# Attention and two MLPs on one core: cluster chain and normalisation one tile sooner, weight conversions in five tiles of twelve

## Chip, cores, metric

One NeuronCore of a Trainium2 chip. The metric is the device time of one execution in microseconds, the median of several runs. Engines are named as in the profile: PE (TensorE matmuls), PEld (its weight loads), DVE (VectorE), ACT (ScalarE), POOL (GpSimd), SP (SyncE, here the only queue that issues DMAs).

## What is computed

```python
# q, k, v: (2, 8, 768, 64); centroids: (8, 16, 64)
q_assign = argmax(einsum('bhsd,hcd->bhsc', q_n, c_n))      # nearest of 16 clusters
k_assign = argmax(einsum('bhsd,hcd->bhsc', k_n, c_n))
scores = where(q_assign[..., None] == k_assign[..., None, :], q @ k.T / 8, -1e9)
x = softmax(scores) @ v                                    # -> (1536, 512)
x = relu(x @ w_in) ** 2 @ w_out                            # 512 -> 2048 -> 512
p = domain_probs / domain_probs.sum(-1)
out = sum over 4 experts of p[:, e] * (relu(x @ w1[e]) @ w2[e])
```

All of it is fp32. Matmuls work on pairs of a rounded value and its remainder (names ending in h and l, or hi and lo), so most operands are made twice.

## The kernel before

The attention is one loop over 96 tiles `g`: 16 heads of 6 tiles, a tile being 128 queries of a head. Twelve tiles make a pair of heads, and a tile is named below by its number and by its place in the twelve (tile 61 is place 1 of its pair, tile 55 is place 7). In each tile PE makes the scores of the tile after next (`S`, L593), transposes the probabilities of the present one in two halves (`T0`, `T1`, L626) and multiplies earlier ones with v (L640, L642). DVE takes the row maximum of the scores (`nb`, L602) and the remainder of each transposed half (`ptl`, L632, two a tile); ACT does the exponential (L613) and the rounded copy of each half (`pth`, L631). The transposed halves go through two PSUM buffers, so T0 of a tile waits for the first `ptl` of the tile before it.

Two strings in `ORDER` (one for even tiles, one for odd) set the order in which a tile's pieces are emitted, and every engine runs its instructions in that order. Beside the base work a tile has places for other work:

- **The slots X1 and X2** take PE work of the cluster chain of the next pair of heads, at places given in `AT` (`START` for the first). Its steps: four transposes of k and q ("t": L364, evacuated by ACT to `kqf`, L371, then split by POOL into `nkh`/`nkl` and `nqh`/`nql`, L52 and L373); two cluster scores, one for each half of the 768 rows ("a", first two: four matmuls each from nkh, nkl, nqh, nql, L414, copied by ACT to `ys`, L420); two turns (transposes of ys, L430, reduced by DVE to `A`, L435); and the one-hot transposes (`pair_hot`, L481). All these use one PSUM buffer, `ps_m`, with bufs=1. `nkh` and its three fellows have one SBUF buffer each.
- **The queue `dq`**, from which C takes one entry: two maxima on DVE (L469, L470), each followed by POOL work (L459 to L467). They make the one-hot rows that the one-hot transposes read.
- **The normalisation** of the pair that has just ended (`norm_steps`, f1 to f5): sums to reciprocals on DVE (L696, L697), a transpose (L702), a store and a broadcast load through DRAM (`rd`, `rb`, L708, L714), and POOL work (f4: L723; f5, two halves: L677, L52, L686).
- **K, the weight conversion**: one entry of `cq`, from tile 8 on, if dq is empty and the tile's place is in "turns". There are 24 entries, four blocks of six: five DVE operations on the scratch tile `cva` (L167, L170, L173, L178, L183) and one copy by ACT with a subtraction by POOL (`w0h`, L189; `w0l`, L191). `cva` has one buffer, so the first operation of a block waits for the `w0l` of the block before. When cq is empty, K loads two weight pieces (`raw`, L109) in each tile whose number is 4 modulo 6.
- **R** issues the DMAs that put the heads' operands together: `k1`, `q1`, `k2`, `q2` (`stack`, L385 and L387, copies out of nkh, nkl, nqh, nql), the one-hot rows (L498), v, and the next q and k.

After the last tile come the two MLPs, dense matmuls from L783 on.

Of the kernel before, what the change touches and what calls it, by code (L numbers as in the profile page):

```python
# [13 lines left out]
AX = mybir.AxisListType  # L14
# [10 lines left out]
    "S T0 X1 M E T1 R Y1 H0 P0 X2 C H1 L0 L1 C K Y2".split(),  # L25
    "S X1 E M T0 T1 Y1 H0 C P1 X2 R L0 H1 C L1 Y2 O K C".split()]
WARM = [12, 10, 5, 11, 3, 9]
START = {'t': [0, 0, 1, 1], 'a': [3, 3, 4, 4, 7], 'stack1': 4, 'stack': 5, 'head': 2, 'gap': 3}
AT = {"gap": 4, "stack1": (-11, -10), "stack": (-9, -9), "ohd": -7, "splitv": -3, "load": -10,
      "t": [-14, -13, -12, -11], "a": [-10, -10, -9, -8, -5], "conv": 8, "turns": (2, 6, 7, 8, 9, 10)}  # L30


@with_exitstack
def moe_attention_kernel(
# [20 lines left out]
    C = centroids.shape[1]  # L55
    NT, DM = out.shape
    E = moe2_w1.shape[0]
    NTT = S // 128
# [147 lines left out]
    with tc.manual_schedule():  # L206
# [217 lines left out]
        def pair_turn(j, half):  # L424

            def f():
                m = ps_m.tile([128, QT, 128], F32, tag="m", name="m")
                for t in range(QT):
                    c0 = half * HALF + t * 128
                    nc.tensor.transpose(m[:, t], ys[j][:, c0:c0 + 128], identf)  # L430

                def evac():
                    if half == 0:
                        ya[j] = as_p.tile([128, 4 * NTT, C], F32, tag="A", name="A")
                    nc.vector.reduce_sum(  # L435
                        out=ya[j][:, half * 4 * QT:(half + 1) * 4 * QT],
                        in_=m.rearrange("p t (g s c) -> p (t g) c s", g=4, s=2), axis=AX.X)
                    if half:
                        for _ in range(len(dq)):
                            dq.pop(0)()  # L440
                        dq.extend(pair_ops(j, ya.pop(j)))
                        for _ in range(2):
                            dq.pop(0)()
                return evac
            return f

        ys, ya = {}, {}

        def pair_ops(j, A):
            mx = as_p.tile([128, 4 * NTT, 1], F32, tag="mx", name="mx")  # L450
            mx2 = as_p.tile([128, 4 * NTT, 1], F32, tag="mx2", name="mx2")
# [3 lines left out]
            V, P = nc.vector, nc.gpsimd  # L455
# [10 lines left out]
                P.tensor_scalar(off, av[:, :, 0], 0.0, -1.0, op0=ALU.min, op1=ALU.max)  # L466
                P.tensor_scalar(oh[:, :, :, 1], off, 1.0, -NEG, op0=ALU.add, op1=ALU.mult)  # L467

            m1 = lambda: V.reduce_max(out=mx, in_=A, axis=AX.X)  # L469
            m2 = lambda: V.reduce_max(out=mx2, in_=A, axis=AX.X)  # L470
            return [m1, p1] + [lambda: None] * (AT if j > 1 else START)["gap"] + [m2, p2]

        def pair_hot(j):

            def f():
                while dq:
                    dq.pop(0)()
                om = oms[j] = as_p.tile([128, HALF], F32R, tag="ohm", name="ohm")
                m = ps_m.tile([128, HALF], F32R, tag="m", name="m")
                for a in range(QT):  # L480
                    nc.tensor.transpose(  # L481
                        m[:, a * 128:(a + 1) * 128],
                        ohs["p", j][:, 2 * a:2 * a + 2].rearrange("p t e s c -> p (t e s c)"), identr)

                def evac():
                    nc.scalar.copy(om, m.bitcast(F32))
                    hot_rows(2 * j)
                return evac
            return f
# [50 lines left out]
        def onehot_slot(i):  # L540

            def f():
                while dq:
                    dq.pop(0)()
                om = as_p.tile([128, HALF], F32R, tag="ohm", name="ohm")[0:4 * C]
                m = ps_m.tile([4 * C, HALF], F32R, tag="m", name="m")
                for a in range(QT):
# [141 lines left out]
        def norm_steps(hp):  # L689
# [36 lines left out]
            def f5(half):  # L726
                norm_scaled(hp, half, st["rb"][:, half * HALF:(half + 1) * HALF], nc.gpsimd, round_pool)

            return [[f1], [], [f2], [], [f3, lambda: f4], [], [lambda: f5(0)], [lambda: f5(1)]]

        def norm_last(hp):
            st = {}
# [339 lines left out]
        split_v(0)  # L1072
        k2hi()
        while dq:
            dq.pop(0)()
        k1lo()
        nc.gpsimd.memset(cp.bitcast(F32), 0.0)
        for e in range(2):
# [11 lines left out]
        emit_max(1)  # L1090
        sums()
        for _ in range(2):
            dq.pop(0)()
        nc.sync.dma_start(out=dp, in_=domain_probs.rearrange("(b p t) e -> p b t e", b=B, t=NTT))
        load_w(*w_loads(0)[0])

# [31 lines left out]
        cq, lq = [], []  # L1128
# [10 lines left out]
        for g in range(NU):  # L1139
# [29 lines left out]
                    f()  # L1169

            def convert():
                if g >= AT["conv"] and cq:
                    if not dq and g % (2 * NTT) in AT["turns"]:
                        cq.pop(0)()
                elif not cq and g % NTT == 4:
                    for _ in range(2):
                        lq and lq.pop(0)()

            def finish(n):
                f = end.pop(n, None)  # L1180
# [8 lines left out]
            def maximum():  # L1189
# [6 lines left out]
                "M": maximum, "P0": lambda: PV(0), "P1": lambda: PV(1),  # L1196
                "O": PO, "R": other, "T0": lambda: T(0), "T1": lambda: T(1),
                "X1": lambda: slot("Y1"), "X2": lambda: slot("Y2"),
                "C": lambda: dq and dq.pop(0)(),
                "K": convert,  # L1200
            }
            for a in ORDER[par]:
# [25 lines left out]
        f1, f2, f3, f4 = norm_last(hp)  # L1228
        f1()
        while dq:  # L1230
            dq.pop(0)()
        act = early_gemm1(1)
        whole(f2)
        act()
# [146 lines left out]
```

## Time and profile before

| | |
|---|---|
| runs, median (lowest, highest) | 1029.36 us (1028.94, 1030.99) |
| the profiled execution: its time, its span | 1029.81 us, 1028.0 us |
| PE busy, PEld busy | 1015.5 us (99%), 899.3 us (87%) |
| DVE, ACT, POOL busy | 675.7 us (66%), 530.2 us (52%), 567.0 us (55%) |
| chain that ended last | PE 85%, DVE 5%, POOL 3%, DMA 2%, ACT 2% |
| granted PE clock | full speed in all 40 slices |

The profile comes from one execution, whose span is the time from its first to its last instruction; the time of the run is 1.8 us longer. PE's busy time is modelled from starts and pipelined ends, so a PE at 99% may still be delayed; whether it is shows in the distance between the starts of matmuls. Below, the one-hot transposes of PE (L481) serve as marks: stretch 1 runs from those of tile 7 to those of tile 19, stretch 6 to those of tile 79, twelve tiles each. In the views times are microseconds from the start of the span, and what stands in brackets at the end of a row is how long its engine was idle before it and what ended that.

### The profile page before, as it was taken

How to read it: one execution, taken by the hardware profiler on the slowest of the kernel's cores; microseconds unless marked ns; L12 is line 12 of the kernel's file. 1: busy time of each engine (PE TensorE's matmuls, PEld its weight loads, DVE VectorE, ACT ScalarE, POOL GpSimd, SP SyncE). 2: the span in 40 equal slices, each digit the busy share in tenths (PEclk: the TensorE clock that was granted, in tenths of full speed). 3: DMA queues.
4: the chain of work that ended last, by engine and by line, in shares of the span. 5: the costliest groups of instructions: out<-in, count | busy, mean ns of one | idle time of the engine just before them, and what ended most of it. 6: DMA issues, size and time to landing. Idle time of an engine off the chain costs nothing.

```text
span 1028.0 us, 14886 instructions
## 1 busy us (share of the span) xinstructions
PE 1015.5 (99%) x5507; PEld 899.3 (87%) x5507; DVE 675.7 (66%) x1047; ACT 530.2 (52%) x1066; POOL 567.0 (55%) x557
## 2 busy tenths in 40 slices
PE   8999999999999999999999999999999999999998
PEld 7988899899888888888889898899888898998887
DVE  8888888889776773721265555578686565555554
ACT  6888888889565533443353343333453333333331
POOL 4467787574232222235456656667678566566550
PEclk9999999999999999999999999999999999999999
DMA  6577766863123320211012212112124122122101
GB/s 151 113 178 179 162 144 156 179 164 90 32 92 98 108 82 31 93 41 41 0 42 83 73 50 82 57 67 83 44 80 143 42 82 83 41 83 69 55 1 62
DMA packets 73745, 88.86 MB, mean 86 GB/s; under 512 B 27252, under 2 KB 50184, under 8 KB 73672
## 3 DMA queue, kind: packets, MB, share of 16 engines
q1 hardware_dynamic: 73672, 87.91, 30.5%
q8 instruction: 43, 0.70, 0.3%
q14 instruction: 30, 0.25, 0.1%
HBM read 62.58 MB, written 3.19 MB: 64 GB/s over the span
## 4 chain that ended last, share of the span: by engine, by line
PE 85%; DVE 5%; POOL 3%; DMA 2%; ACT 2%; issue 1%; SPq 1%; POOLq 0%; ACTq 0%
PE bank L954 25%; PE bank L914 22%; PE bank L807 13%; PE bank L783 4%; PE bank L784 4%; PE bank L782 4%; PE s L593 3%; PE t L626 3%; PE po L640 2%; PE po L642 2%; DVE ptl L632 1%; DVE nb L602 1%; DMA rd<-rt 1%; DMA rb<-rd 1%; POOL nql L373 1%
## 5 line engine op out<-in xcount | busy, mean ns | idle before, releaser
L954 PE MATMUL bank<-w1h,ga 128*128 128x512 f32 x768 | 269.9, 393 | 0.0
L964 DVE SCALAR_TENSOR_TENSOR x<-bank,pe_p,x 128x512 f32<-128x512 f32 x180 | 135.0, 751 | 167.7 <-PE bank L954 167.6
L914 PE MATMUL bank<-xa,w0h 128*128 128x384 f32 x896 | 228.3, 335 | 0.1
L914 PEld LDWEIGHTS bank<-xa,w0h 128*128 128x128 f32 x896 | 164.5, 188 | 17.9 <-ACT fa L925 0.5
L954 PEld LDWEIGHTS bank<-w1h,ga 128*128 128x128 f32 x768 | 144.1, 188 | 24.5
L793 POOL TENSOR_TENSOR ga<-fa,ga 128x512 fp32r<-128x512 f32 x48 | 63.2, 1318 | 177.7 <-ACT ga L792 136.7
L954 PE MATMUL bank<-w1l,ga 128*128 128x512 f32 x384 | 151.6, 395 | 0.0
L914 PE MATMUL bank<-xa,w0l 128*128 128x384 f32 x448 | 149.7, 334 | 0.0
L925 ACT COPY fa<-bank 128x384 f32<-128x384 f32 x96 | 45.5, 474 | 171.7 <-PE bank L914 171.7
L807 PE MATMUL bank<-ga,w1h 128*128 128x512 f32 x384 | 126.6, 389 | 0.0
L934 ACT ACTIVATE ga<-fa 128x384 fp32r<-128x384 f32 x96 | 50.5, 527 | 135.6 <-DVE fa L928 135.6
L883 POOL TENSOR_TENSOR w0l<-raw,w0h 128x512 fp32r<-128x512 f32 x64 | 75.0, 1195 | 81.4 <-ACT w0h L882 81.4
L901 POOL TENSOR_TENSOR w1l<-raw,w1h 128x1024 fp32r<-128x1024 f32 x32 | 77.3, 2414 | 71.3 <-ACT w1h L900 71.3
L632 DVE TENSOR_TENSOR ptl<-t,pth 128x384 fp32r<-128x384 f32 x192 | 97.8, 548 | 26.7 <-ACT pth L631 26.4
L602 DVE TENSOR_REDUCE nb<-s 128x1 f32<-128x768 f32 x96 | 91.3, 951 | 7.9 <-PE s L593 6.9
L937 DVE SCALAR_TENSOR_TENSOR ga<-fa,ga 128x384 fp32r<-128x384 f32 x96 | 90.1, 938 | 0.6 <-ACT ga L934 0.6
L631 ACT CAST pth<-t 128x384 fp32r<-128x384 f32 x192 | 84.5, 486 | 8.8 <-PE t L626 8.1
L613 ACT ACTIVATE p<-s,nb 128x768 f32<-128x768 f32 x96 | 87.7, 914 | 2.0 <-DVE nb L602 1.9
L626 PE MATMUL t<-identf,p 128*128 128x128 f32 x576 | 86.7, 276 | 1.3 <-DVE ptl L632 0.8
L593 PE MATMUL s<-k,q 80*128 80x384 f32 (+1 forms) x384 | 85.7, 344 | 2.2 <-DMA k<-ohm 1.4
L790 ACT ACTIVATE fa<-bank 128x512 f32<-128x512 f32 x44 | 26.3, 598 | 116.3 <-PE bank L784 116.3
L807 PEld LDWEIGHTS bank<-ga,w1h 128*128 128x128 f32 x384 | 72.0, 188 | 14.7
(213 smaller groups left out, 2045.1 us busy)
## 6 DMA issues: line engine op xcount, KB each, us to landing
raw<-in_moe_w_dram SPq DMA_DIRECT2D x64, 512.0 KB, 4.3
raw<-in_moe_w_in_dram SPq DMA_DIRECT2D x7, 1024.0 KB, 5.2
raw<-in_moe_w_out_dram SPq DMA_DIRECT2D x6, 1024.0 KB, 4.9
k<-nkh SPq DMA_DIRECT2D x28, 192.0 KB, 3.8
q<-nqh SPq DMA_DIRECT2D x28, 192.0 KB, 3.9
nv<-in_v_dram SPq DMA_DIRECT2D x16, 192.0 KB, 3.9
out_dram<-x SPq DMA_DIRECT2D x12, 256.0 KB, 2.1
k<-nkl SPq DMA_DIRECT2D x14, 192.0 KB, 3.3
```

The costliest lines, as they stand in the source:

```text
L593: nc.tensor.matmul(s[:, j, 0:HALF], stk[i, nq][:, t * 128:(t + 1) * 128], stk[i, nk][:, j * HALF:(j + 1) * HALF], start=first, stop=not first)
L602: nc.vector.tensor_reduce(out=nb, in_=s_ps[u][:, :, 0:HALF], axis=AX.XY, op=ALU.max, negate=True)
L613: nc.scalar.activation(p, s_ps.pop(u)[:, :, 0:HALF], AF.Exp, bias=nb_t.pop(u), accum_out=sums_t[hp][:, i % 2, t:t + 1])
L626: nc.tensor.transpose(tp[:, j], p_sb[u][:, half, j * 128:(j + 1) * 128], identf)
L631: return (lambda: nc.scalar.copy(dh, tp), lambda: nc.vector.tensor_tensor(dl, tp, dh.bitcast(F32), op=ALU.subtract))
L632: lambda: nc.vector.tensor_tensor(dl, tp, dh.bitcast(F32), op=ALU.subtract))
L807: nc.tensor.matmul(o, a, b, start=(ft == 0 and z == 0), stop=(ft == NF - 1 and z == 2))
L901: nc.gpsimd.tensor_tensor(lo, w, hi.bitcast(F32), op=ALU.subtract)
L914: nc.tensor.matmul(ps, w[:, o:o + 128], r_op(r, x)[:, kt], start=(first and kt == 0 and z == 0), stop=(kt == 1 and z == 2), skip_group_che ...
L937: nc.vector.scalar_tensor_tensor(out=g_t(n, f, t, 1), in0=h_src(n, f, t), scalar=0.0, in1=g_t(n, f, t, 0).bitcast(F32), op0=ALU.max, op1=A ...
L954: nc.tensor.matmul(o, a, w[:, f], start=(f == 0 and z == 0), stop=(f == 1 and z == 2))
L964: nc.vector.scalar_tensor_tensor(out=acc, in0=o, scalar=pc, in1=acc, op0=ALU.mult, op1=ALU.add)
```

## The change

The places of the cluster chain become 1, 2, 2, 3, 7 instead of 2, 2, 3, 4, 7: the first cluster scores go to the tile that also has the fourth transpose, the first turn to the tile of the second scores. The maxima of the queue keep to places 4 and 5. `norm_steps` drops one empty step, so that the broadcast load and f5 come one tile sooner (places 5, 7 and 8 instead of 6, 8 and 9), and f4 runs in place 6, in its slot. Conversions run at places 6 to 10 and no longer at 2. Pieces of weights are loaded at place 10, two at a time, the first four as soon as half of the conversions are done.

```diff
-AT = {"gap": 4, "stack1": (-11, -10), "stack": (-9, -9), "ohd": -7, "splitv": -3, "load": -10,
-      "t": [-14, -13, -12, -11], "a": [-10, -10, -9, -8, -5], "conv": 8, "turns": (2, 6, 7, 8, 9, 10)}
+AT = {"stack1": (-11, -10), "stack": (-9, -9), "ohd": -7, "splitv": -3, "load": -10,
+      "t": [-14, -13, -12, -11], "a": [-11, -10, -10, -9, -5], "conv": 8, "turns": (6, 7, 8, 9, 10)}
...
                     if half:
-                        for _ in range(len(dq)):
-                            dq.pop(0)()
-                        dq.extend(pair_ops(j, ya.pop(j)))
-                        for _ in range(2):
-                            dq.pop(0)()
+                        first, second = pair_ops(j, ya.pop(j))
+                        if j == 1:
+                            first()
+                            dq.extend([None] * 3 + [second])
+                        else:
+                            dq.extend([None, first, None, None, None, second])
...
-            return [[f1], [], [f2], [], [f3, lambda: f4], [], [lambda: f5(0)], [lambda: f5(1)]]
+            return [[f1], [], [f2], [f3], [f4], [lambda: f5(0)], [lambda: f5(1)]]
...
             def convert():
-                if g >= AT["conv"] and cq:
-                    if not dq and g % (2 * NTT) in AT["turns"]:
-                        cq.pop(0)()
-                elif not cq and g % NTT == 4:
+                turn = g % (2 * NTT)
+                if g >= AT["conv"] and cq and not dq and turn in AT["turns"]:
+                    cq.pop(0)()
+                if lq and turn == AT["turns"][-1] and len(cq) <= (12 if len(lq) > 4 else 0):
                     for _ in range(2):
-                        lq and lq.pop(0)()
+                        lq.pop(0)()
```

`first` is the first maximum with its POOL work, `second` the second.

**PE, tiles 61 and 62 (places 1 and 2): the first cluster scores.** In these rows `m<-nkh` to `m<-nql` are the scores of one half, `t` is T0, `s` the scores of attention. Before:

```order
L640 MATMUL po<-pth,vv 128x256
L642 MATMUL po<-ptl,vv 128x256
L593 MATMUL s<-k_2502,q_2596 128x384 x2
L593 MATMUL s<-k_2599,q_2601 128x384 x2
L626 MATMUL t<-identf,p 128x128 x3
L414 MATMUL m<-nkh,cp 128x384
L414 MATMUL m<-nkl,cp 128x384
L414 MATMUL m<-nqh,cp 128x384
L414 MATMUL m<-nql,cp 128x384
```

With the change:

```order
L651 MATMUL po<-pth,vv 128x256
L653 MATMUL po<-ptl,vv 128x256
L419 MATMUL m<-nkh,cp 128x384
L419 MATMUL m<-nkl,cp 128x384
L419 MATMUL m<-nqh,cp 128x384
L419 MATMUL m<-nql,cp 128x384
L604 MATMUL s<-k_2508,q_2605 128x384 x2
L604 MATMUL s<-k_2608,q_2610 128x384 x2
L637 MATMUL t<-identf,p 128x128 x3
```

The first scores now stand at the end of tile 61, ahead of S and T0 of tile 62. The second scores take their old place behind T0, and the first turn stands at the end of tile 62.

**POOL, the second pair (tiles 18 to 22): f4, the conversion's subtraction and f5.** `xs<-xs,xm` is f4, `rb` and `xa` are f5. Before:

```order
L723 TENSOR_TENSOR xs<-xs,xm 128x384 x2
L191 TENSOR_TENSOR w0l<-cva,w0h 128x4x128
L677 TENSOR_TENSOR rb<-rb,xs 128x384
L52 TENSOR_SCALAR xa<-rb 128x384
L686 TENSOR_TENSOR xa<-rb,xa 128x384
```

With the change:

```order
L734 TENSOR_TENSOR xs<-xs,xm 128x384 x2
L688 TENSOR_TENSOR rb<-rb,xs 128x384
L52 TENSOR_SCALAR xa<-rb 128x384
L697 TENSOR_TENSOR xa<-rb,xa 128x384
L688 TENSOR_TENSOR rb<-rb,xs 128x384
L52 TENSOR_SCALAR xa<-rb 128x128
L697 TENSOR_TENSOR xa<-rb,xa 128x128
L52 TENSOR_SCALAR xa<-rb 128x256
L697 TENSOR_TENSOR xa<-rb,xa 128x256
L191 TENSOR_TENSOR w0l<-cva,w0h 128x4x128
L52 TENSOR_SCALAR vv<-nv 128x6x64
```

`w0l` has gone from ahead of f5 to behind it, and the conversion that writes `cva` anew stands one tile later on DVE (tile 21). In the third pair `w0l` stands behind `vv` (tile 33, the next block begins in tile 34), in the fourth between the first `nkl` and the second `nkh` (tile 46), the last one in tile 66.

**DVE, tiles 62 to 64 of the sixth pair: the turns.** `A<-m` ends a turn, `mx` is the first maximum. Before:

```order
L602 TENSOR_REDUCE nb<-s 128x1
L435 TENSOR_REDUCE A<-m 128x192
L696 TENSOR_SCALAR r<-sums 128x12
L632 TENSOR_TENSOR ptl<-t,pth 128x3x128
L697 RECIPROCAL r<-r 128x12
L632 TENSOR_TENSOR ptl<-t,pth 128x3x128
L602 TENSOR_REDUCE nb<-s 128x1
L435 TENSOR_REDUCE A<-m 128x192
L469 TENSOR_REDUCE mx<-A 128x24
L632 TENSOR_TENSOR ptl<-t,pth 128x3x128 x2
```

With the change:

```order
L643 TENSOR_TENSOR ptl<-t,pth 128x3x128 x2
L440 TENSOR_REDUCE A<-m 128x192
L613 TENSOR_REDUCE nb<-s 128x1
L440 TENSOR_REDUCE A<-m 128x192
L707 TENSOR_SCALAR r<-sums 128x12
L643 TENSOR_TENSOR ptl<-t,pth 128x3x128
L708 RECIPROCAL r<-r 128x12
L643 TENSOR_TENSOR ptl<-t,pth 128x3x128
L613 TENSOR_REDUCE nb<-s 128x1
L476 TENSOR_REDUCE mx<-A 128x24
L643 TENSOR_TENSOR ptl<-t,pth 128x3x128 x2
```

The first `A` is taken at the end of tile 62, behind both its `ptl`; in tile 64 one reduction stands ahead of the `ptl` instead of two.

On SP the pieces of weights (L109) stood in tile 64 between a load of v and the store `rd` of the normalisation; now none do so. They stand behind the load of v in tiles 34, 46, 70 and 82.

## Rows read from the trace of the kernel before

**Rows 1.** Busy time by stage: the attention loop (us, each engine's busy us and count).

```profile
19.60:253.30 233.70, 228.79 (x1691) 212.13 (x1691) 202.50 (x346) 201.45 (x478) 153.51 (x214) 1.00 0.65 150
```

**Rows 2.** Timeline of PE: one-hot transposes, the marks of stretches 1 to 6 (start, length).

```profile
40.30 0.28 PE L481 MATMUL m<-identr,oh 128*128 128x128 f32 x1
...
70.77 0.29 PE L481 MATMUL m<-identr,oh 128*128 128x128 f32 x2
...
102.55 0.23 PE L481 MATMUL m<-identr,oh 128*128 128x128 f32 x1
...
133.40 0.29 PE L481 MATMUL m<-identr,oh 128*128 128x128 f32 x2
...
163.98 0.29 PE L481 MATMUL m<-identr,oh 128*128 128x128 f32 x2
...
193.89 0.29 PE L481 MATMUL m<-identr,oh 128*128 128x128 f32 x2
...
225.68 0.29 PE L481 MATMUL m<-identr,oh 128*128 128x128 f32 x2
```

**Rows 3.** Timeline of PE, tiles 62 and 63: scores, cluster scores, first turn.

```profile
178.77 0.87 PE L593 MATMUL s<-k,q 128*128 128x384 f32 x4
...
179.73 0.42 PE L414 MATMUL m<-nkh,cp 128*128 128x384 f32 x1
...
180.35 0.33 PE L414 MATMUL m<-nql,cp 128*128 128x384 f32 x1
...
183.00 0.55 PE L430 MATMUL m<-identf,ys 128*128 128x128 f32 x3
```

**Rows 4.** Timeline of POOL: the first nkh in stretches 1 to 5.

```profile
51.75 0.51 POOL L52 TENSOR_SCALAR nkh<-kqf 128x384 fp32r<-128x384 f32 x1 [9.68 <-DMA k<-nkh]
...
83.58 0.51 POOL L52 TENSOR_SCALAR nkh<-kqf 128x384 fp32r<-128x384 f32 x1
...
114.39 0.52 POOL L52 TENSOR_SCALAR nkh<-kqf 128x384 fp32r<-128x384 f32 x1 [1.10 <-ACT p L613]
...
144.94 0.51 POOL L52 TENSOR_SCALAR nkh<-kqf 128x384 fp32r<-128x384 f32 x1 [0.86 <-ACT p L613]
...
175.34 0.51 POOL L52 TENSOR_SCALAR nkh<-kqf 128x384 fp32r<-128x384 f32 x1 [0.98 <-ACT xo L664]
```

**Rows 5.** Timeline of POOL, 165 to 182 us: ahead of and behind the nkh at 175.34.

```profile
165.74 1.29 POOL L191 TENSOR_TENSOR w0l<-cva,w0h 128x512 fp32r<-128x512 f32 x1
...
173.35 1.01 POOL L305 TENSOR_TENSOR vv<-nv,vv 128x384 fp32r<-128x384 f32 x1
...
179.09 1.01 POOL L373 TENSOR_TENSOR nql<-kqf,nqh 128x384 fp32r<-128x384 f32 x1
```

**Rows 6.** Timeline of SP, 164 to 173 us: the last copy out of nkh.

```profile
171.13 0.87 SPq L385 DMA_DIRECT2D k<-nkh  x1
```

**Rows 7.** Timeline of DVE, 181 to 188.6 us: tile 62's ptl, then the first A.

```profile
181.61 1.02 DVE L632 TENSOR_TENSOR ptl<-t,pth 128x384 fp32r<-128x384 f32 x2 [0.97 <-ACT pth L631]
183.16 0.96 DVE L602 TENSOR_REDUCE nb<-s 128x1 f32<-128x768 f32 x1 [0.52 <-PE s L593]
184.03 0.55 DVE L435 TENSOR_REDUCE A<-m 128x192 f32<-128x384 f32 x1
```

**Rows 8.** Timeline of ACT, 164 to 167 us: the conversion's copy.

```profile
165.03 0.63 ACT L189 CAST w0h<-cva 128x512 fp32r<-128x512 f32 x1
```

**Rows 9.** Timeline of POOL at 76 us: f5 of the second pair begins.

```profile
75.97 1.01 POOL L677 TENSOR_TENSOR rb<-rb,xs 128x384 f32<-128x384 f32 x1 [2.14 <-DMA rb<-rd]
```

**Rows 10.** Instructions on cva: first operation of a block (ns min/median/max, first and last start).

```profile
L167 DVE TENSOR_SCALAR cva<-raw x18: 412/416/429, 43.8 to 431.8; 128x512 int32<-128x512 int32 x18
```

**Rows 11.** Waits of PEld in the attention loop (total us, times, longest).

```profile
PEld t L626 <- DVE ptl L632: 9.3, 35, 0.5
```

**Rows 12.** Timeline of SP, 188 to 200 us: two weight pieces ahead of rd.

```profile
189.23 1.40 SPq L109 DMA_DIRECT2D raw<-in_moe_w_out_dram  x2
```

**Rows 13.** Timeline of PE, 198 to 201 us: S of tile 70.

```profile
200.46 0.59 PE L593 MATMUL s<-k,q 80*128 80x384 f32 x2 [1.43 <-DMA k<-ohm]
```

More of the change, by code (lines that the diff above doesn't have):

```diff
@@ L27 @@
 WARM = [12, 10, 5, 11, 3, 9]
-START = {'t': [0, 0, 1, 1], 'a': [3, 3, 4, 4, 7], 'stack1': 4, 'stack': 5, 'head': 2, 'gap': 3}
-AT = {"gap": 4, "stack1": (-11, -10), "stack": (-9, -9), "ohd": -7, "splitv": -3, "load": -10,
-      "t": [-14, -13, -12, -11], "a": [-10, -10, -9, -8, -5], "conv": 8, "turns": (2, 6, 7, 8, 9, 10)}
+START = {'t': [0, 0, 1, 1], 'a': [3, 3, 4, 4, 7], 'stack1': 4, 'stack': 5, 'head': 2}
+AT = {"stack1": (-11, -10), "stack": (-9, -9), "ohd": -7, "splitv": -3, "load": -10,
+      "t": [-14, -13, -12, -11], "a": [-11, -10, -10, -9, -5], "conv": 8, "turns": (6, 7, 8, 9, 10)}
 @with_exitstack
@@ L297, in moe_attention_kernel, with step @@
         dq = []
+        def step():
+            f = dq.pop(0)
+            if f:
+                f()
         def split_v(i):
@@ L467, in p2, with first, second @@
                 P.tensor_scalar(oh[:, :, :, 1], off, 1.0, -NEG, op0=ALU.add, op1=ALU.mult)
-            m1 = lambda: V.reduce_max(out=mx, in_=A, axis=AX.X)
-            m2 = lambda: V.reduce_max(out=mx2, in_=A, axis=AX.X)
-            return [m1, p1] + [lambda: None] * (AT if j > 1 else START)["gap"] + [m2, p2]
+            def first():
+                V.reduce_max(out=mx, in_=A, axis=AX.X)
+                p1()
+            def second():
+                V.reduce_max(out=mx2, in_=A, axis=AX.X)
+                p2()
+            return first, second
         def pair_hot(j):
@@ L476, in f @@
                 while dq:
-                    dq.pop(0)()
+                    step()
                 om = oms[j] = as_p.tile([128, HALF], F32R, tag="ohm", name="ohm")
@@ L543, in f @@
                 while dq:
-                    dq.pop(0)()
+                    step()
                 om = as_p.tile([128, HALF], F32R, tag="ohm", name="ohm")[0:4 * C]
@@ L1074, in moe_attention_kernel @@
         while dq:
-            dq.pop(0)()
+            step()
         k1lo()
@@ L1092, in moe_attention_kernel @@
         for _ in range(2):
-            dq.pop(0)()
+            step()
         nc.sync.dma_start(out=dp, in_=domain_probs.rearrange("(b p t) e -> p b t e", b=B, t=NTT))
@@ L1198, in moe_attention_kernel @@
                 "X1": lambda: slot("Y1"), "X2": lambda: slot("Y2"),
-                "C": lambda: dq and dq.pop(0)(),
+                "C": lambda: dq and step(),
                 "K": convert,
@@ L1230, in moe_attention_kernel @@
         while dq:
-            dq.pop(0)()
+            step()
         act = early_gemm1(1)
```

## Prediction

> **What bounds the kernel now.** I read the busy time by stage first. In the attention loop PE is busy for 228.8 of 233.7 us [rows 1], DVE and ACT for 86 to 87% of it: nothing has much room, and what PE loses it loses in short waits. So I read the loop by its twelve-tile stretches, from mark to mark [rows 2]: 30.47, 31.78, 30.85, 30.58, 29.91 and 31.79 us. Then PE within one stretch: where it reaches the cluster scores, and whether their inputs are there. Then POOL, which makes those inputs, and the copy that lets POOL begin. The table of PEld's waits says how much PE loses to DVE.
>
> In stretch 5 the chain that matters runs beside PE. The one-hot rows leave PE at 163.98; from there SP issues copies one behind the other (four of one-hot rows, xm, two of k1, two of q1), and the copy of k2 out of nkh is issued at 171.13 [rows 6], 7.15 us after the mark. POOL may overwrite nkh when that copy has landed. It does so at 175.34, after 0.98 us of idling [rows 4], though its last vv had ended at 174.36 [rows 5] and kqf was long there; in stretch 1 the row names the copy itself. So the first nkh comes 11.45, 12.81, 11.84, 11.54 and 11.36 us after the mark [rows 2, 4]; only in stretch 2 POOL was not idle before it. From the first nkh to the end of the first nql are 4.76 us (175.34 to 180.10) [rows 4, 5]. PE issues the matmul on nql at 180.35 [rows 3]: the inputs were ready 0.25 us before. The chain and PE arrive together.
>
> **The change, part by part.**
>
> *First scores one tile sooner.* They now begin where tile 62's S began, at 178.77, 14.79 us after the mark, and reach nql 0.62 us later (179.73 to 180.35) [rows 3], so at 15.4. The copies that free nkh hang on the mark, not on the tile in which they are emitted; their order on SP is unchanged, and so is POOL's 4.76 us. Nql is there at 11.4 + 4.8 = 16.2. PE waits where it had not waited, and what was gained by coming sooner is lost. f5 one tile sooner doesn't help: POOL was idle before nkh.
>
> *From the first nql to the next mark.* Before: 193.89 - 180.35 = 13.54 us in a stretch with no conversions behind the scores. Now S and T0 of the tile follow the scores as well: + 0.96 (178.77 to 179.73) [rows 3].
>
> *The turns.* ps_m is one buffer, so the second turn waits until DVE has reduced the first. That reduction stands behind both ptl of tile 62, which ended at 182.63, 3.86 us into the tile; + 0.55 [rows 7] + 0.1 to start PE gives 4.5. PE used to reach its first turn 4.23 us into the tile (183.00) [rows 3], with both scores behind it; the first turn costs about 0.35 us less than the second scores (0.7), so it comes to the second turn at 3.9. A new wait of 0.6, of which 0.05 I count as margin: + 0.55. Bounds: 0, if the ptl end sooner, and 1.1, if DVE comes a conversion late. On the other side T0 of the tile after A and mx waits no longer: such waits are 0.5 at most [rows 11]; - 0.4. The first maximum and f4 cost nothing: they stay under the same base work.
>
> So from the first nql to the mark it is 13.54 + 0.96 + 0.55 - 0.4 = **14.65 us**, and a stretch takes (first nkh after the mark) + 4.85 + 14.65.
>
> *Conversions.* No conversion at place 2 is a gain that is already in the 13.54 (stretch 5 had none there). What is new is where w0l stands. In stretch 2 it stands behind f5 on POOL, and f5 cannot begin before the broadcast has landed: 75.97 [rows 9], a time that SP's queue sets. f5 ended about 82.0 (83.58 less some 1.6 for vv [rows 4, 5]), so w0l ends at 83.3 with its 1.29 [rows 5]. But the next block's first operation is in DVE's queue already in tile 21 and writes cva: DVE stands still until 83.3, and behind it nb and ptl. Then 0.42 [rows 10], 0.87 for nb (183.16 to 184.03) and 0.5 for a ptl [rows 7]: T0 of tile 23 can go at 85.1. With the mark at 40.30 + 30.95 = 71.25 PE would reach it after 0.2 + three tiles of 2.43 (14.58 / 6) + 0.71, at 79.45. It waits 5.65 us; the first nql comes at 15.4 + 5.65 = 21.05, later than its inputs. Bounds: 0, if the broadcast lands 5 us sooner, and 6.5.
>
> In stretch 3 vv ended 10.74 us after the mark (114.39 less 1.10) [rows 2, 4]; w0l, formerly ahead of f5, is now behind vv, so it ends there, and T0 of tile 36 goes at 10.74 + 0.42 + 0.87 + 0.5 = 12.5, against 10.6 by PE's pace: 1.9, nql at 17.3. In stretch 4 w0l is put between the first nkl and the second nkh: + 1.29 on the way to nql. In tile 66 it meets nothing.
>
> *Pieces of weights.* In stretch 6 two pieces of 1.40 us stood ahead of the store rd [rows 12], so the broadcast and behind it the one-hot rows came late, PE waited 1.43 us for them [rows 13], and POOL's chain was late too. They are gone from there: stretch 6 takes what stretch 5 takes. At their new places a load of v and copies needed a tile later or more stand around them; before, the pieces of tile 58 stood the same way, in the shortest stretch: nothing.
>
> **The sum.** Stretch 1: 11.45 + 19.5 = 30.95, + 0.48. Stretch 2: 21.05 + 14.65 = 35.7, + 3.9. Stretch 3: 17.3 + 14.65 = 31.95, + 1.1. Stretch 4: 11.54 + 1.29 + 19.5 = 32.33, + 1.75. Stretch 5: 11.36 + 19.5 = 30.86, + 0.95. Stretch 6: 30.86, - 0.93. Together + 7.25; what lies before and after (first pair, last pair, both MLPs) issues the same work in the same order but for pieces loaded earlier: 0. The profiled execution took 1029.81, which gives 1037.06; it stood 0.45 above the median of the runs, so I say **1036.6 us**, slower by 0.7%.
>
> **The rivals.**
>
> *The chain does not hold the scores* (about 1030.0). If the copy landed as soon as POOL has finished vv, at 9.1 us (10.38 less the 1.29 of w0l that is no longer there), nql would be ready at 14.0 and PE would come first: at 14.8 where ACT's copy w0h, 0.63 us [rows 8], is gone from the way (stretches 1, 5, 6), else at 15.4. Stretches: - 1.02, + 3.9, + 1.1, - 0.53, - 0.46, - 2.34: + 0.65. Against it: in three of the stretches POOL idles 0.86 to 1.10 us with everything but nkh's release at hand [rows 4]. The Trainium skill (DMA: Bandwidth & Descriptors, Anatomy of one DMA — SWDGE (gpsimd) path) puts a DMA, on that path, at about 2.0 us fixed plus its bytes at 436 GB/s, some 2.5 us for the 192 KB here as an estimate; by that rule the release comes at 9.6 and this rival is the forecast. The trace disagrees: from issue to the first nkh it is 4.21 us [rows 4, 6].
>
> *DVE's lateness is what counts* (about 1021, faster). PE loses 9.3 us to ptl [rows 11]. If spreading the chain takes two thirds of that away (6.2) and nothing takes their place, with some 2.0 us from the store in stretch 6, the sum is - 8.2. It decides if the first nkh starts before 9.9 us after the mark and w0l is written before the next block asks for cva. For it: the busy share of DVE; and the waits are real. Against it: rows 4, and the place of w0l on POOL.
>
> *Within the forecast*, without the wait of the turns (6 x 0.55) and with w0l early (- 2.6 in stretch 2, then bound by its chain at 13.6 + 19.5 = 33.1): 1030.5. With 1.1 for the turns: 1040.
>
> **How the numbers follow.** Forecast 0.70, chain not holding 0.14, DVE alone 0.11, 0.05 for more delay than I see (a DVE held up again by cva). Range: it leaves out the fast rival and some 0.07 above: 1029.0 to 1040.0. 0.2%, or 2.1 us, is about what a measurement of this kernel can tell from no change. Faster: 0.12. Same: 0.15, the first rival and a little of the forecast's low end. Slower: 0.73.
>
> **What would show it.** Marks 30.9 to 32.3 us apart, but about 35.7 in stretch 2; a wait of PE on nql of about 1 us at the end of places 1; a wait on A between S and the second turn at places 3; in tile 21 DVE idle for 5 us or more with POOL's w0l as its releaser; in stretch 6 no wait for one-hot rows. The forecast is wrong if the first nkh starts before 10 us after the mark, or if DVE does not idle in tile 21.

## The result and the profile after

The changed kernel is slower by 1.0%: 1040.71 us (median of four runs; 1039.04 to 1041.22, and one of 2036.47) against 1030.17 (1028.94 to 1031.50), ratio 1.0097 with a 95% interval of 1.0074 to 1.0119. Executions whose granted clock was low from end to end, or that took a multiple of the others' time, are in no ratio, and profiles of that kind are not read. The profiled execution took 1040.20 us, its span is 1038.4, 10.4 more than before. The forecast was 1036.6, 1029.0 to 1040.0: the sign was right, the size too small by 4.1 us, and the time lies 0.7 above the range.

The busy times by stretch, from mark to mark, of the changed kernel (us, then each engine's busy us and count for PE, PEld, DVE, ACT and POOL, PE's granted clock, DMA share, GB/s):

```profile
39.61:70.83 31.22, 29.86 (x224) 28.01 (x223) 25.50 (x46) 25.74 (x62) 14.09 (x20) 1.00 0.73 174
70.83:107.00 36.17, 30.93 (x224) 29.25 (x223) 27.45 (x48) 26.50 (x64) 22.50 (x31) 0.95 0.61 139
107.00:139.34 32.34, 30.11 (x225) 27.73 (x224) 27.42 (x47) 26.63 (x64) 22.50 (x31) 1.00 0.68 159
139.34:173.66 34.32, 31.79 (x224) 29.30 (x223) 27.06 (x47) 26.21 (x64) 22.66 (x31) 0.95 0.70 162
173.66:204.88 31.22, 29.86 (x225) 27.78 (x224) 28.14 (x47) 26.15 (x64) 21.64 (x30) 1.00 0.64 141
204.88:236.07 31.19, 29.83 (x225) 27.95 (x223) 24.95 (x43) 25.98 (x63) 21.80 (x31) 1.00 0.62 156
```

Beside the stretches of before [rows 2], of the forecast, and of two runs that are told below:

| stretch | before | forecast | after | chain and maxima back | six turns |
|---|---|---|---|---|---|
| 1 | 30.47 | 30.95 | 31.22 | 29.94 | 31.23 |
| 2 | 31.78 | 35.7 | 36.17 | 39.48 | 31.53 |
| 3 | 30.85 | 31.95 | 32.34 | 31.97 | 31.88 |
| 4 | 30.58 | 32.33 | **34.32** | 31.82 | 31.97 |
| 5 | 29.91 | 30.86 | 31.22 | 29.91 | 31.19 |
| 6 | 31.79 | 30.86 | 31.19 | 29.88 | 31.04 |
| sum | 185.38 | 192.65 | 196.46 | 193.00 | 188.84 |

The six stretches took 11.1 us more; everything outside them 842.62 before and 841.94 after. So the whole loss is in the chain's stretches, and two things stand out: stretch 4, and a clock of 0.95 in stretches 2 and 4, where before it was 1.00 throughout.

The waits in the loop, 40 to 236 us (total us, times, longest):

```profile
POOL nkh L52 <- DMA k<-nkh: 12.7, 3, 9.7
PEld t L637 <- DVE ptl L643: 12.6, 22, 4.7
...
DVE cva L167 <- POOL w0l L191: 6.9, 2, 5.4
...
PEld m L435 <- DVE A L440: 3.9, 6, 0.7
PEld m L419 <- POOL nqh L52: 3.2, 3, 1.9
PEld m L419 <- POOL nql L378: 2.9, 4, 0.9
```

Three of these did not stand in the table of before: DVE on w0l, the second turn on A, and PE on nqh. PEld's wait on ptl [rows 11] grew in its longest from 0.5 to 4.7.

**Stretch 1: the chain holds the scores.** The timeline of SP, with the copy of k2 out of nkh:

```profile
46.83 0.88 SPq L390 DMA_DIRECT2D k<-nkh  x1
```

The timeline of POOL, first nkh and first nql:

```profile
51.06 0.52 POOL L52 TENSOR_SCALAR nkh<-kqf 128x384 fp32r<-128x384 f32 x1 [9.67 <-DMA k<-nkh]
...
54.82 1.00 POOL L378 TENSOR_TENSOR nql<-kqf,nqh 128x384 fp32r<-128x384 f32 x1
```

The timeline of PE, end of tile 13:

```profile
54.79 0.45 PE L419 MATMUL m<-nqh,cp 128*128 128x384 f32 x1 [0.34 <-POOL nqh L52]
55.87 0.44 PE L419 MATMUL m<-nql,cp 128*128 128x384 f32 x1 [0.63 <-POOL nql L378]
56.15 0.86 PE L604 MATMUL s<-k,q 128*128 128x384 f32 x4
```

POOL stood idle for 9.67 us until the copy out of nkh had landed, 11.45 us after the mark, to the hundredth what it was before [rows 2, 4]. Nql was ready 4.76 us later (54.82 + 1.00). PE, now a tile sooner at its scores, waits for nqh and for nql. Its matmul on nql starts 16.26 us after the mark; in this stretch of before it started 16.25 after it. So coming a tile sooner gained nothing, and from there to the next mark are 14.96 us where 14.22 were enough.

**Stretch 2: DVE waits behind the normalisation.** The timeline of POOL:

```profile
74.92 1.01 POOL L688 TENSOR_TENSOR rb<-rb,xs 128x384 f32<-128x384 f32 x1 [2.46 <-DMA rb<-rd]
...
80.66 1.26 POOL L191 TENSOR_TENSOR w0l<-cva,w0h 128x512 fp32r<-128x512 f32 x1
```

Of DVE:

```profile
81.96 0.72 DVE L167 TENSOR_SCALAR cva<-raw 128x512 int32<-128x512 int32 x1 [5.36 <-POOL w0l L191]
```

Of PE, tile 23:

```profile
84.06 1.54 PE L637 MATMUL t<-identf,p 128*128 128x128 f32 x6 [4.51 <-DVE ptl L643]
...
85.61 0.41 PE L653 MATMUL po<-ptl,vv 128*128 128x256 f32 x1
85.83 0.41 PE L651 MATMUL po<-pth,vv 128*128 128x256 f32 x1
```

The broadcast lands, f5 runs, w0l runs behind it, and only then the next block may write cva. DVE had been idle for 5.36 us, PE for 4.51. Then a thing that no row of before shows: the matmuls on v start 0.21 to 0.22 us apart, where they were 0.12 apart in the tile before. From T0 to the end of the tile are 2.62 us (84.06 to 86.68); two tiles later the same matmuls take 1.37 (90.22 to 91.59). The granted clock falls here: it is 0.66 in the row from 84.50 to 88.00 below.

**Stretch 4: w0l in the chain, and the clock.** The timeline of POOL:

```profile
151.44 0.51 POOL L52 TENSOR_SCALAR nkh<-kqf 128x384 fp32r<-128x384 f32 x1 [1.81 <-ACT p L624]
...
153.01 1.28 POOL L191 TENSOR_TENSOR w0l<-cva,w0h 128x512 fp32r<-128x512 f32 x1
...
156.41 1.00 POOL L378 TENSOR_TENSOR nql<-kqf,nqh 128x384 fp32r<-128x384 f32 x1
```

Of PE, tiles 49 and 50:

```profile
156.38 0.44 PE L419 MATMUL m<-nqh,cp 128*128 128x384 f32 x1 [1.55 <-POOL nqh L52]
157.47 0.46 PE L419 MATMUL m<-nql,cp 128*128 128x384 f32 x1 [0.64 <-POOL nql L378]
...
159.37 0.52 PE L419 MATMUL m<-nkl,cp 128*128 128x384 f32 x1
159.69 0.52 PE L419 MATMUL m<-nqh,cp 128*128 128x384 f32 x1
160.01 0.52 PE L419 MATMUL m<-nql,cp 128*128 128x384 f32 x1
```

And the busy times (columns as above) behind the wait of stretch 2 and around that of tile 49:

```profile
84.50:88.00 3.50, 3.50 (x21) 3.47 (x20) 2.99 (x5) 2.54 (x8) 2.26 (x3) 0.66 0.29 63
...
155.00:157.00 2.00, 0.44 (x1) 0.19 (x1) 0.12 (x1) 0.00 (x0) 1.92 (x3) 1.00 0.45 98
157.00:159.00 2.00, 1.53 (x9) 1.50 (x9) 0.33 (x1) 1.04 (x3) 1.92 (x4) 0.88 0.44 98
159.00:161.00 2.00, 2.00 (x10) 1.90 (x9) 0.62 (x1) 1.04 (x4) 1.48 (x2) 0.50 0.57 128
161.00:163.00 2.00, 2.00 (x14) 2.00 (x13) 1.30 (x3) 1.70 (x5) 0.00 (x0) 0.76 0.93 229
```

PE waits 1.55 and 0.64 us with one matmul between; then its granted clock falls to 0.50, the lower of its two levels (1.2 instead of 2.4 GHz), and the cluster scores of tile 50 start 0.32 us apart, where those of tile 38 stand 0.18 apart (125.84, 126.02, 126.20). Tile 50 takes 4.61 us (157.76 to 162.37); the same tile of the other pairs takes 3.03 to 3.05. That is 1.6 us more, behind waits of 2.2. Tile 51 gives some back (2.73 instead of 3.08 to 3.10), and from the matmul on nql to the mark the stretch takes 16.19 us, 1.2 more than stretches 1, 5 and 6 (14.96 to 15.00).

### The profile page after: what moved, and what is told of

It reads as the page before. It is cut to its first block, busy times and chain, and to the rows that moved or that the text cites. A ratio compares the mean times of both kernels' runs of the same rounds, so it can differ in the third digit from the quotient of the medians.

```text
span 1038.4 us, 14897 instructions
## 1 busy us (share of the span) xinstructions
PE 1016.5 (98%) x5507; PEld 901.7 (87%) x5507; DVE 676.1 (65%) x1047; ACT 528.8 (51%) x1066; POOL 567.5 (55%) x557
## 4 chain that ended last, share of the span: by engine, by line
PE 81%; DVE 3%; DMA 1%; SPq 1%; ACT 1%; POOL 1%; issue 1%; POOLq 0%; ACTq 0%
PE bank L965 25%; PE bank L925 22%; PE bank L818 13%; PE bank L794 4%; PE bank L793 4%; PE bank L795 4%; PE t L637 2%; PE s L604 2%; PE po L651 1%; PE po L653 1%; DVE ptl L643 1%; DVE nb L613 1%; PE m L419 1%; PE s L793 0%; DMA k<-nkh 0%
```

## The experiments

My theory after the result was that of the forecast plus the clock: nkh's release holds the first scores; w0l behind f5 or between nkh and nql costs what the table shows; a long wait brings the lower clock on top. The rivals: the place of the scores is worth nothing and the order of the conversions everything, or the reverse; DVE's waits only move on; the clock has nothing to do with the waits. Each kernel is the changed one with one thing altered, where nothing else is said. Ratios are to the kernel before. Of long lines an edit shows only the part that changes.

**The scores a tile later again.**

```diff
-"a": [-11, -10, -10, -9, -5]
+"a": [-10, -10, -9, -8, -5]
```

> Kernel: the changed kernel, with only the cluster scores, their turns and the one-hot rows back at the tiles of before (scores one tile later, second turn in the tile after the first). Theory (nkh's release by the k2 copy holds the first scores, about 11.4 us after the mark, and 4.8 us later nql; coming a tile sooner only adds 0.96 of work and 0.6 of a wait between the turns behind it): stretches 1, 5 and 6 fall from 31.2 to about 30.0, stretch 4 from 34.3 to 32 or 33 (33 if the half-clock piece at 158 to 162 us comes back), stretch 2 stays above 35 because DVE still waits for w0l in tile 21, stretch 3 falls to about 31.6. Sum about -7: 1033. The wait of the second turn on A (0.7 us in each place 3) is gone. Rival (the order of the conversions is what costs, the place of the scores costs nothing): 1039 to 1041, stretches 1, 5 and 6 within 0.3 us of the changed kernel's.

1042.64 us, ratio 1.012 (1.0103 to 1.0137): no gain at all, since a wait of another kind had come, on the one-hot rows at every mark (table of waits, 40 to 238 us):

```profile
PEld m L492 <- POOL oh L473: 9.0, 6, 1.8
```

The changed kernel takes its two maxima out of the queue later than the kernel before did; with the second turn a tile later the second maximum is only made when the one-hot transposes ask for it. PE's wait of the second turn on A was gone as expected, and its waits on nqh and nql fell from 4.1 to 1.3 us, but this run can't settle the price. So the maxima had to go back too:

```diff
-dq.extend([None, first, None, None, None, second])
+first()
+dq.extend([None] * 4 + [second])
```

> Kernel: the changed kernel, with cluster scores, turns, one-hot rows and the two maxima all where they were before; only the conversions, the normalisation and the weight pieces stay changed. (With the scores alone put back, the second maximum came too late and PE waited 1.65 to 2.1 us for the one-hot rows at every mark.) Theory: that wait goes with the maxima; stretches 1, 5 and 6 are 29.5 to 30.0, stretch 2 about 35.6 (DVE's wait on w0l in tile 21 stays), 3 about 30.2, 4 about 31.6, so the sum is 10 below the changed kernel's: 1029.5 to 1031, no different from before, the loss in stretch 2 set against what stretch 6 gains. Rival (the place of the scores and maxima is worth nothing either way, the conversions cost it all): 1037 to 1041.

1036.93 us, ratio 1.0061 (1.0044 to 1.0079). The stretches are read from one more execution of this kernel:

> Kernel: the run with scores, turns, one-hot rows and maxima back and all else changed, profiled once more, since the granted clock was 0.85 all through its first profile. Its times (1036.2 to 1037.1) lie 6 us above the theory's. If the conversions make the rest, stretch 2 is 36 to 37 with a stretch at the lower clock behind the wait on w0l in tile 21, stretches 3 and 4 are 31.5 to 32.5 and stretches 1, 5 and 6 are at 29.5 to 30. If instead the place of the scores is worth nothing, stretches 1, 5 and 6 are at 31.

1037.22 us, a single execution. Its busy times by stretch:

```profile
40.11:70.05 29.94, 29.70 (x223) 28.02 (x223) 25.60 (x46) 26.08 (x62) 14.08 (x20) 1.00 0.79 181
70.05:109.53 39.48, 31.98 (x225) 29.88 (x224) 27.53 (x48) 26.84 (x64) 22.41 (x31) 0.91 0.56 129
109.53:141.50 31.97, 29.88 (x224) 27.79 (x223) 27.40 (x47) 26.93 (x64) 22.65 (x31) 1.00 0.72 165
141.50:173.32 31.82, 30.30 (x225) 27.83 (x223) 27.41 (x47) 26.57 (x64) 23.12 (x31) 1.00 0.70 161
173.32:203.23 29.91, 29.86 (x224) 27.80 (x223) 27.09 (x47) 26.30 (x64) 21.66 (x30) 1.00 0.72 161
203.23:233.11 29.88, 29.61 (x224) 27.93 (x223) 25.02 (x43) 26.30 (x63) 21.75 (x31) 1.00 0.63 157
```

In the stretches that only the chain sets, 1, 5 and 6, the earlier chain with its maxima cost 1.28, 1.31 and 1.31 us: the first part of the theory, and the rival that its place costs nothing falls. The matmul on the first nql starts 16.27, 16.23 and 16.22 us after the mark here and 16.26, 16.24 and 16.19 in the changed kernel. Only what follows it differs: 13.66 to 13.68 us here, 14.96 to 15.00 there. Why the run as a whole stayed 6 us above my number is mostly stretch 2 (39.48 for 35.6; stretch 3 was 1.8 above it too), with the store of the reciprocal sums and the broadcast behind it (SP's timeline):

```profile
67.76 0.39 SPq L716 DMA_DIRECT2D rd<-rt  x1
71.77 1.11 SPq L722 DMA_DIRECT2D rb<-rd  x2
```

The broadcast is issued when the store has landed, 4.0 us after its issue here and 3.1 in the changed kernel. With the mark sooner the rest is later against it: f5 begins 6.95 us after the mark instead of 4.09, DVE waits 8.2 us for w0l, PE also 1.9 for one-hot rows, and the clock is at half for over 6 us. In the expectation I had priced this stretch as if the broadcast came with the mark; it comes with SP's queue.

**The copy of k2 ahead of those of q1.**

```diff
-("q1", 128, qh, qh), ("k2", D + C, kh, None),
+("k2", D + C, kh, None), ("q1", 128, qh, qh),
```

> Kernel: the changed kernel, with the copy of k2 out of nkh issued ahead of the two copies of q1 instead of behind them. Nothing else moves. Theory: k2 is issued about 1.5 us sooner, nkh is free about 1.5 us sooner (9.9 us after the mark instead of 11.4 in stretches 1, 5, 6 and 10.5 instead of 12.1 in stretch 4), PE no longer waits on nqh and nql at places 1 of tiles 13 and 73 (1.5 us each) and waits less in tile 49 (2.8 us now). Stretches 1 and 6: -1.2 each, 4: -1.5 or more (more if the shorter wait leaves the clock at its upper level), 5: -0.1, since DVE's waits already make PE late there, 2 and 3: 0, the wait on w0l comes first. Sum -4 to -5.5: 1035 to 1037. Rival (DMA queues deliver k2 at the same time whatever its place, or POOL's own work holds nkh): 1040 to 1041, first nkh within 0.3 us of the changed kernel's in every stretch.

1037.42 us, ratio 1.0071 (1.0055 to 1.0088). The timeline of SP in stretch 1:

```profile
45.55 0.55 SPq L390 DMA_DIRECT2D k<-nkh  x1
```

And of POOL:

```profile
49.44 0.51 POOL L52 TENSOR_SCALAR nkh<-kqf 128x384 fp32r<-128x384 f32 x1 [7.74 <-ACT pth L642]
```

Nkh comes 9.51 us after the mark instead of 11.45, and stretches 1, 6 and 4 become 29.73, 29.63 and 31.74: 1.49, 1.56 and 2.58 less. The rival that the place of the copy is nothing falls. Stretch 4 gained 1.2 more than nkh (1.35 sooner), and its clock stayed at 1.00: in tile 49 PE went from the matmul on nkl to S in 1.81 us instead of 3.27. Stretch 5 stayed at 31.23: nkh came at 11.48 there, since POOL itself was at vv until then. Stretches 2 and 3 took back 2.05 and 0.46, where I had said 0: the marks came sooner, the broadcast did not (75.19 instead of 74.92).

**Conversions begun two tiles sooner.**

```diff
-"conv": 8
+"conv": 6
```

> Kernel: the changed kernel, with the weight conversions begun two tiles sooner (tile 6 instead of 8), so that w0l falls in tiles 18, 31, 44 and 57 instead of 20, 33, 46 and 66; the last two pairs of weight pieces come one pair of heads earlier. Theory (what costs in stretch 2 is that w0l stands behind the normalisation while the next block's first operation waits for it, in stretch 4 that w0l stands between nkl and nkh): DVE's 5.4 us wait on w0l and PE's 5.9 us in tile 23 are gone, with the half-clock stretch behind them; first nkh in stretch 2 at 11.4 instead of 12.7; stretches 2 to 4 come down to 31 to 31.8 each, like 1, 5 and 6. Sum -8 to -9.5: 1031 to 1032.5. What stays above before is the chain. Rival A (DVE's waits only move to other tiles): 1037 or more. Rival B (the half clock has nothing to do with PE's waits): the waits go, but granted clock below 1.0 stays in stretches 2 and 4.

1036.55 us, ratio 1.0058 (1.0038 to 1.0078). Stretches 2 and 3 came down to 31.43 and 31.82 at a clock of 1.00, as the theory said; stretch 4 went up to 34.85, with this row in DVE's timeline:

```profile
144.07 0.72 DVE L167 TENSOR_SCALAR cva<-raw 128x512 int32<-128x512 int32 x1 [3.64 <-POOL w0l L191]
```

W0l now falls into tile 44, where POOL puts it behind f5, and the next block asks for cva in tile 45. It is the wait of stretch 2 over again: rival A for this stretch, and the clock followed the wait (147 to 151 us at about half). Rival B falls: where the wait is gone the half clock is gone, where it moved the clock moved with it.

**A sixth tile of conversions in a pair**, so that w0l always falls at place 7, ahead of f5.

```diff
-"turns": (6, 7, 8, 9, 10)
+"turns": (6, 7, 8, 9, 10, 11)
...
-if lq and turn == AT["turns"][-1] and
+if lq and turn == 10 and
```

> Kernel: the changed kernel, with a sixth tile of conversions in a pair (places 6 to 11) so that a block takes exactly one pair of heads: w0l always falls at place 7, ahead of the normalisation on POOL, and the next block's first operation one place later; the pieces stay at place 10. Theory: no wait of DVE on w0l in any stretch, no half clock, w0l never between nkh and nql; stretches 2 to 4 become 31.3 to 31.8, the others stay at 31.2, held by nkh's release at 11.4: sum 188 to 189 against 196.5, 1032 to 1033. What is left above before is the chain. Rival (five operations in a row make DVE late in the tile that follows place 11, or the waits on w0l move on as they did with the earlier start): 1035 or more, with DVE idle over 1.5 us at some w0l.

1033.25 us, ratio 1.0032 (1.0020 to 1.0043). DVE no longer waits on w0l. The busy times of stretches 2 to 4:

```profile
71.21:102.74 31.53, 30.38 (x224) 27.85 (x223) 27.46 (x48) 26.30 (x64) 23.13 (x31) 1.00 0.67 153
102.74:134.62 31.88, 30.21 (x224) 27.93 (x223) 27.12 (x48) 26.34 (x64) 22.58 (x31) 1.00 0.69 164
134.62:166.59 31.97, 30.25 (x224) 27.96 (x223) 27.19 (x48) 26.37 (x64) 22.61 (x31) 1.00 0.71 171
```

The order of the conversions is worth 7.5 us of the changed kernel's time, 4.6 in stretch 2, 0.5 in stretch 3 and 2.4 in stretch 4. In stretch 4 nql ends 1.13 us sooner and the stretch is 2.35 shorter; the 1.2 between is the clock's.

**The weight pieces alone, on the kernel before.**

```diff
-elif not cq and g % NTT == 4:
+if lq and g % (2 * NTT) == 10 and len(cq) <= (12 if len(lq) > 4 else 0):
```

> Kernel: the kernel before, with only the weight pieces moved to the tenth tile of a pair (34, 46, 58, 70) instead of 58, 64, 70, 76. Theory (the two pieces ahead of the store of the reciprocal sums made stretch 6 long): stretch 6 falls from 31.8 to 29.9 to 30.1, the other stretches stay within 0.3; 1028.2 to 1028.6, faster by 0.15 to 0.2%. PE's wait of 1.4 us for the one-hot rows in tile 70 is gone. Rival (pieces meet as much at the new places): 1030 to 1031, and one of the stretches 3, 4 or 5 longer by over 0.5.

1028.37 us, ratio 0.9982 (0.9973 to 0.9992). Stretch 6 is 29.79, 2.0 less. SP's timeline ahead of it now has

```profile
190.14 0.81 SPq L708 DMA_DIRECT2D rd<-rt  x1
194.06 1.11 SPq L714 DMA_DIRECT2D rb<-rd  x2
```

instead of two pieces ahead of the store [rows 12] and a broadcast at 195.62. This part of the change pays by itself. Leaving place 2 without conversions saved time too: from the first nql to the next mark stretches 1 to 4 took 14.18 to 14.22 us before, and 13.54 to 13.69 in the run with chain and maxima back; stretch 5, which had no conversion there before, has 13.54 and 13.68. Stretches 2 and 3 were 0.6 and 0.8 longer in this execution, and a longer stretch 3 was the rival's sign. The rows show other reasons than a piece. In stretch 2, which has none, the broadcast was issued 1.53 us after the mark instead of 0.99. In stretch 3 the copy of k2 was issued 8.42 us after it instead of 7.63, with the issue of two one-hot copies (2.31 us instead of 1.28) ahead of it; the pieces stand behind that copy.

**Both repairs together: six turns and k2 first.**

> Kernel: as the run with six turns, and the copy of k2 issued ahead of the copies of q1. Theory (the two costs add up, and once nkh comes free sooner the earlier scores are a gain): stretches 1, 4, 5 and 6 are 29.6 to 29.8, where PE itself reaches nql; stretch 2 is about 31.4 (POOL's normalisation is late there), 3 about 30.5. Sum 180 to 181.5 against 185.4 before: 1025 to 1026.5, faster than before by 0.4%. Rival (DVE or the wait between the turns takes what the chain gives back): 1028 to 1031.

1030.41 us, ratio 1.0002 (0.9993 to 1.0012), a miss by 4 us. Stretches 3 to 6 are 31.09, 30.75, 30.13 and 29.67, up to 1.0 above what I said; stretch 2 is 34.70, 3.3 above. SP's timeline there:

```profile
68.08 0.42 SPq L719 DMA_DIRECT2D rd<-rt  x1
73.05 1.11 SPq L725 DMA_DIRECT2D rb<-rd  x2
```

The store took 5.0 us to land, the one-hot rows behind the broadcast were late, and PE waited 2.2 us for them in tile 22. And without the change, k2 first together with the pieces, on the kernel before:

> Kernel: the kernel before, with the weight pieces at the tenth tile of a pair and the copy of k2 issued ahead of the copies of q1. Theory (with the scores a tile later PE and the chain arrive together, within 0.3 us, so a sooner release helps little): stretches 1, 4, 5 and 6 gain 0.1 to 0.3 each on the run with the pieces alone, stretch 3 gains 1.0 to 1.4 (its nkh came at 12.6), stretch 2 nothing (POOL is late). 1026 to 1027.5. Rival (the place of the copy is worth its 1.5 us in every stretch): 1021 to 1022. Other rival (worth nothing): 1028 to 1029.

1027.43 us, ratio 0.9972 (0.9963 to 0.9981), in the range, but partly by luck. Against the run with the pieces alone stretch 1 gained 1.0 us where I had 0.1 to 0.3 and stretch 3 gained 1.6; stretch 4 lost 1.0, since the store there took 5.1 us to land and the broadcast was issued 0.45 us after the mark.

**The four early weight loads out of the way of that store.** They stood in tiles 12 to 15.

```diff
-at(early, 2 * NTT + kk, lambda kk=kk: load_in(kk))
+at(early, 3 * NTT + 4 + kk // 2, lambda kk=kk: load_in(kk))
```

> Kernel: as the run with six turns and the k2 copy first, and the four loads of in_moe_w_in that stood in tiles 12 to 15 now in tiles 22 and 23. What it tests: stretch 2 was 34.7 us in that run because the store rd came behind those loads and landed 5 us after its issue (68.08 to 73.05), so the broadcast and the one-hot rows behind it on SP came late (PE waited 2.4 us in tile 22 and 2.0 us in tile 25). Theory: the store goes at about 64, stretch 2 comes down to 30.5 to 31.2, the others stay; sum 182 to 182.8, 1026 to 1027. Rival (the loads hold up as much in their new tiles, or the landing of rd is slow for another reason): 1029 to 1031, stretch 2 above 33.

1029.62 us, ratio 0.9991 (0.9977 to 1.0004); expected were 1026 to 1027, and the rival's 1029 to 1031 is what came. No trace of this kernel can be set beside the others by stretch, so where the rest lies stays open. The same with chain and maxima back:

> Kernel: as the run with the early loads moved, but scores, turns, one-hot rows and maxima back at the tiles of before. It compares the two places of the chain where nkh's release and the conversions no longer hold anything up. Theory: the later place is still the better one, by the 0.6 us of the wait between the turns in each of six stretches, and because nql is there 0.3 us before PE rather than after it: stretches 29.5 to 30.0, sum 178 to 179.5, 1022.5 to 1024.5, 2.5 to 4 us less than with the scores early. Rival (with the chain free, sooner is better or the same): no less than the run with the early scores, 1026 to 1028.

1025.86 us, ratio 0.9964 (0.9951 to 0.9976). Stretches 1, 2, 4, 5 and 6 are 29.42 to 29.97, as expected; stretch 3 is 32.78, since there the store rd landed 4.1 us after its issue (96.18 to 100.30) and the broadcast was issued 0.67 us after the mark; that is the miss. By the ratios the later scores are better by 2.8 us, and their intervals only just part. And the kernel before with the three cheap edits (pieces, k2 first, early loads):

> Kernel: the kernel before, with the weight pieces at the tenth tile, the k2 copy first and the four early loads in tiles 22 and 23; chain, normalisation and conversions as before. Theory: stretch 2, 31.8 in the run without the loads moved, becomes 30.0 to 30.4; stretch 4, 31.5 there because the broadcast landed late, is not touched by it. 1025.5 to 1026.5. Rival (nothing gained: nkh is late in stretch 2 for POOL's own work): 1027 to 1028.

1026.29 us, ratio 0.9958 (0.9945 to 0.9971); stretch 2 is 29.97 (31.80 with the loads in place), as expected. The total is in the range by luck in part: stretch 3, 30.01 with the loads in place, is 32.01 now, with the broadcast issued 1.01 us after the mark, and stretch 4, 31.48 there, is 30.04. These two beat both kernels, and can't be told apart from each other.

## Why the prediction was right in sign and short in size

- **First scores one tile sooner.** Right. The first nkh came 11.45, 12.67, 12.52, 12.10, 11.41 and 11.39 us after the marks. It moves with the copy of k2, not with the tile, and the earlier place with its maxima costs 1.3 us a stretch.
- **From the first nql to the next mark, 14.65.** Too small by 0.3: 14.96 in stretch 1 (55.87 to 70.83), 14.98 and 15.00 in 5 and 6. The work of the tile was right to a tenth; 0.12 is PE's restart, since S follows the matmul on nql by 0.28 where it is released late and by 0.17 where not. In six stretches this is nearly 2 us, half of the miss.
- **The turns.** Right: the second turn waits 0.70 where 0.10 was lost before (+ 0.60 for + 0.55), place 5 lost 0.16 instead of 0.50 (- 0.35 for - 0.4).
- **Conversions, stretch 2.** The mechanism was right, to the tile and the releaser; DVE idled 5.36 us. The length, 36.17 for 35.7, came close because errors cancelled: w0l ended 1.4 us sooner than I had it (81.92 for 83.3), and some 1.2 us of half clock in tile 23 were not in the sum.
- **Stretch 3.** The mechanism was right: DVE waited 1.55 us for w0l behind vv, PE 1.22 for ptl, and PE's matmul on nql started 17.44 us after the mark where I said 17.3; the rest is the 0.3. But I had not seen that the copy of k2 would be late here (nkh at 12.52), so that nql was ready only 0.14 us ahead of PE. Without the wait on w0l, in the run with six turns, the stretch is still 31.88.
- **Stretch 4, "+ 1.29 on the way to nql".** This is the step that failed. W0l stood where I said, but the copy landed 0.56 later (nkh at 12.10 for 11.54), and **a longer wait of PE is not worth its length**: the clock fell to its lower level behind it. The matmul on nql started 18.13 us after the mark for 17.68, and from there to the next mark were 16.19 us for 14.65: the 0.3 of every stretch and 1.2 of the clock. The forecast had 32.33, the trace 34.32. It had put the clock at nothing without a reason, although its own sum held a wait of PE of 5.65 us in stretch 2.
- **Pieces of weights.** Right for stretch 6, alone 2.0 us.
- The six misses, 0.27, 0.47, 0.39, 1.99, 0.36 and 0.33, make 3.8; the first mark came 0.7 sooner, for no reason that I looked into. That leaves 3.1 between the two profiled executions. The other 1.0 of the 4.1 is a matter of the execution read: the forecast took off 0.45 because the profiled one of before stood above its median, and the one of after stands 0.51 below its own (1040.20, 1040.71).

Of the rivals, *the chain does not hold the scores* fell by the run with k2 first: the earlier copy alone took 1.5 and 1.6 us off stretches 1 and 6. In stretch 1 nkh came 11.45 us after the mark, 4.23 us after the issue of the copy. The rule of the Trainium skill (DMA: Bandwidth & Descriptors, Anatomy of one DMA — SWDGE (gpsimd) path), which is given for DMAs on GpSimd's path while SP issued this one, would have freed it at 9.6 as an estimate; the trace disagrees. *DVE's lateness is what counts* fell by its own conditions: nkh came at 11.4 and not before 9.9, and DVE waited for w0l. With six turns w0l is there in time, and PEld's waits on ptl fall from 8.1 us in the six stretches of before to 4.1; the stretches are 3.5 us longer all the same, since PE then waits for the chain. The lower price *within the forecast* adds up to 1030.7, not 1030.5; nothing hangs on it. The range was too narrow above because its upper end held a longer wait between the turns and nothing for the clock. In stretches 2 and 4 the granted clock fell behind PE's waits (0.66 from 84.50 to 88.00, 0.50 from 159.00 to 161.00). The Trainium skill (TensorE: Matmul & The Clock Gate, Part 1) says that PE's clock follows how busy PE has lately been; the trace agrees.

## What to carry to other kernels

A step that is moved sooner gains nothing if what releases its input hangs on a mark and not on the step: follow the release (here a copy in a DMA queue) before you price the move, and move that. An operation that recycles a single buffer holds up the whole in-order engine behind it, so place the last reader of that buffer ahead of slow work on the reader's queue. Where a new wait takes TensorE to a standstill for 1.5 us or more, price it once with and once without the lower clock behind it; a fall cost about 1.2 us here.

## What the runs showed of the hardware that I had not expected

The clock fell to half for 3 to 7 us behind waits of PE of 4.5 us (stretch 2), of 1.6 and 0.6 us close together (stretch 4), of 2.8 us (stretch 4 with the conversions two tiles sooner) and of 1.6 us (72 us, in the run with the scores alone put back). It did not behind waits of 2.5 us (tile 36 with k2 first) and 2.2 us (tile 22 with six turns and k2 first), nor at the other five marks of the run with the scores put back, after waits of 1.1 to 1.3 us. The length of one wait doesn't tell, so for waits of 1.5 to 3 us both prices belong in the range.

The same store of 12 x 128 values landed 2.7 to 5.1 us after its issue ahead of stretches 2 to 6 (67.80 to 70.49 with six turns, 126.61 to 131.74 with pieces and k2 first on the kernel before). SP issues the broadcast when the store has landed, and the one-hot copies behind it. What a late landing cost hung on the mark. In the four kernels with k2 first and no wait on w0l (six turns, pieces, late scores, kernel before with the loads moved) the five stretches in which the broadcast was issued after the mark took 31.48 to 34.70 us, and the fifteen others 29.41 to 31.09. A landing of 4.96 us that left the broadcast 0.64 us ahead of the mark cost nothing (stretch 6 with late scores, 29.42). No run varies the landing alone, so why it varies stays open.
